# Linear attention and a top-128 expert layer on one core: the first six groups in a shorter software pipeline, the first batch's ranks from column sums, the expert's weights loaded later

## The chip, the core and the metric

The kernel runs on one core of one Trainium2 chip. The metric is the device time of one execution in microseconds; three runs of the kernel before gave 183.13, 183.86 and 184.06, the median is 183.86. The engines named below are PE (TensorE matmul; PEld is its weight load), DVE (VectorE), ACT (ScalarE), POOL (GpSimd) and SP (SyncE, which here issues most of the DMAs).

## What is computed

Four batches, eight heads, 768 rows of 64 values, all in float32. The first half is linear attention with a decay per head, in blocks of 64 rows; the second half takes its output as a row of 512 values per token, scores each token, and sends the 128 best tokens of each batch through a two-layer network whose result is added to them.

```python
# per block of 64 rows, state starts at 0
intra = einsum(q k^T) * Dmask ;  intra = einsum(intra, v)
inter = einsum(q * lam_pow, kv_state)
out   = intra + inter
kv_state = lam_block * kv_state + einsum(k * rev_pow, v)
# then, per batch, on x = out as [768, 512]
scores = x @ w_gate ;  top = the 128 highest
x[top] += sigmoid(scores[top]) * (relu(x[top] @ w1) @ w2)
```

## The kernel before, in words

The work is cut into 24 groups of 128 rows (two blocks c = 0, 1), six per batch: group g is tile t = g % 6 of batch g // 6. Each group goes through the same pieces, each a small function:

- `load(g)` issues three DMAs on SP (q, k and v, 256 KB each). A pool keeps seven groups. In the first part of the kernel `fetch_in` makes each load wait until the load three before it has landed (line 69).
- `transposes(g)` turns q and k on PE (L219, L233) into two PSUM banks, and ACT copies them to `qkT` (L224, L238, or L243 when k's half goes to the tail of the `pu` banks). `keys_decayed(g)` (L205) and `queries_decayed(g)` (L270) multiply by powers of the decay on POOL; they make `kd` and `qs`.
- `scores(g)` (L285), `from_states(g)` (L345) and `from_scores(g)` (L356) are the attention's matmuls into `po`; `masked(g)` (L292, DVE) makes `p`, which `from_scores(g)` reads. `state_products(g)` (L308) needs `kd` and fills `pu`; `next_state` adds the decayed state on DVE, either from a product that `decay_state` made on POOL (L318, then L335) or folded into four DVE instructions (L330).
- `outputs(g)` copies the result with three ACT instructions (L370, L372) and stores it (L382, on SP); batch 1 is stored later.
- `gate_scores(g)` (L395, DVE) computes the token scores from the stored row. `row(g)` turns the score column into a row (L418, PE; L421, ACT; L424, DVE), and `compare(g)` counts by DVE instructions (L434) how many tokens beat each token. `compare_older(g)` counts against the older groups of the batch.
- After a batch `plan(b)` hands out its expert work: `ranks` (L470, L475), `tokens` (L486, L492, L495), `fetch` (an indirect DMA on POOL, L509), `gate` (L519, L528), eight hidden pieces (L547), eight back pieces (L561) and `write` (L577, an indirect DMA on POOL). Each is bound by hand to a step; `counts` says how many of the 16 pieces go to each of the steps from 7 on.

The order is written out by hand, and each engine runs its own list in that order. The main loop has one step per group. In step g the kernel finishes group g (`from_scores`, `outputs`), scores group g + 1 and prepares group g + 2. There are three variants. Steps 0 to 5 begin with the transposes of group g + 2 and the score row of group g - 1, which step g then compares; step 6 does the row and comparison of group 5, then ranks, tokens and fetch of batch 0, before `masked(7)`; from step 7 on the transposes come after `state_products`, and the expert's pieces come behind them. Until step 12 a group's `kd` is made at the beginning of the step that uses it in `state_products`; from step 12 on one step earlier (line 748).

The loop that all steps share, cut:

```python
            if g + 2 < NG:
                if g <= FED:
                    keys_decayed(g + 2)
                decay_state(2 * g + 4)
            ...
            from_scores(g)
            outputs(g)
            ...
            if g % NT and lead:
                in_order(pieces)
```

The functions concerned, with their line numbers:

## Time and profile before

| what | value |
|---|---|
| median of three runs | 183.86 us |
| the profiled execution's own time | 182.03 us |
| its span in the profile | 180.2 us |
| PE, PEld, DVE, ACT, POOL busy | 149.8, 119.5, 111.5, 68.9, 96.2 us |
| mean granted TensorE clock | 0.974 |
| moved by DMA | 31.99 MB, mean 177 GB/s |

The span covers the program's instructions; the execution's time has some 1.8 us around them. "Busy" is the union of an engine's instructions. Step g below begins where `from_scores(g)` starts on PE; in this profile the steps 0 to 16 begin at 17.54, 22.05, 26.48, 30.91, 35.36, 39.06, 43.80, 51.82, 61.07, 66.91, 72.17, 77.04, 82.56, 87.75, 92.20, 99.19 and 103.67 us. The last group's step begins at 145.86, and the last expert ends at 176.

### The profile page before, as it was taken

What the parts mean: (1) busy time and instruction counts of PE and PEld (TensorE: products, weight loads), DVE (VectorE), ACT (ScalarE), POOL (GpSimd) and SP (SyncE); (2) the same over time, 40 slices, a digit from 0 to 9 for tenths busy, and PEclk for the clock granted to TensorE, in tenths of its full rate; (3) what the DMA queues carried; (4) which work ended last, traced back from release to release, by engine and by line L of the source; (5) the groups of instructions that cost most, each with busy time, mean ns of one, the idle gap of its engine ahead of it and who ended that gap; (6) DMA issues with size and microseconds to landing.
All of it is one profiled execution on the core that took longest, in us unless ns stands there. A gap on an engine that the chain in (4) does not pass through costs nothing.

```text
span 180.2 us, 8244 instructions
## 1 busy us (share of the span) xinstructions
PE 149.8 (83%) x3586; PEld 119.5 (66%) x3586; DVE 111.5 (62%) x378; ACT 68.9 (38%) x178; POOL 96.2 (53%) x100
## 2 busy tenths in 40 slices
PE   0799777776497999999977989989999997989980
PEld 0568666665386999776655668977666896459620
DVE  4814788899844445768996583589865779330010
ACT  2214555562144344644552552563343641011100
POOL 4358666945074665569786967867574600220002
PEclk9999999999859999999999999999999999999997
DMA  4999798999999998987999999989112131011001
GB/s 97 205 226 219 195 261 221 235 276 307 289 248 272 208 275 180 199 181 174 262 242 290 225 253 245 256 215 238 62 64 62 62 125 50 7 55 58 0 0 58
DMA packets 83381, 31.99 MB, mean 177 GB/s; under 512 B 75665, under 2 KB 79761, under 8 KB 83346
## 3 DMA queue, kind: packets, MB, share of 16 engines
q1 hardware_dynamic: 82560, 29.37, 67.8%
q0 software_dynamic: 640, 2.10, 3.4%
q8 instruction: 28, 0.46, 1.1%
q14 instruction: 7, 0.06, 0.1%
q10 hardware_dynamic: 146, 0.01, 0.0%
HBM read 24.12 MB, written 7.34 MB: 175 GB/s over the span
## 4 chain that ended last, share of the span: by engine, by line
PE 55%; issue 16%; DVE 14%; POOL 6%; DMA 4%; ACT 2%; POOLq 1%; ACTq 0%
PE py L561 10%; PE ph L547 9%; PE pu L308 6%; PE po L356 6%; PE po L345 5%; PE po L285 5%; DVE cmp L434 5%; PE tq L219 5%; POOL qs L270 2%; POOL decayed L318 2%; DMA qn<-in_q_dram 2%; DVE state L335 2%; DMA out_dram<-y,tok 2%; PE tqk L257 2%; DVE p L292 2%
## 5 line engine op out<-in xcount | busy, mean ns | idle before, releaser
L270 POOL TENSOR_TENSOR qs<-qkT,qpow 128x512 f32<-128x512 f32 x24 | 33.0, 1377 | 16.9 <-ACT qkT L224 9.5
L318 POOL TENSOR_TENSOR decayed<-state,decay 128x256 f32<-128x256 f32 x34 | 28.9, 849 | 23.1 <-DVE state L335 10.8
L547 PE MATMUL ph<-xsT,w_sb 128*128 128x128 f32 x256 | 31.1, 278 | 0.7 <-ACT xsT L523 0.7
L547 PEld LDWEIGHTS ph<-xsT,w_sb 128*128 128x128 f32 x256 | 29.5, 192 | 2.5 <-ACT qkT L264 1.2
L561 PE MATMUL py<-w_sb,hs 128*128 128x512 f32 x64 | 30.0, 602 | 0.1
L434 DVE TENSOR_SCALAR_CACHE_REDUCE cmp<-sc_row,sc 128x128 bf16<-128x128 f32 (+4 forms) x65 | 29.8, 503 | 0.0
L205 POOL TENSOR_TENSOR kd<-kn,kpow 128x512 f32<-128x512 f32 x24 | 25.8, 1074 | 4.9 <-DMA kn<-in_k_dram 4.9
L335 DVE TENSOR_TENSOR state<-pu,decayed 128x256 f32<-128x256 f32 x34 | 14.3, 422 | 16.3 <-ACT qkT L243 4.5
L395 DVE CUSTOM_DVE_ANT_0 xg<-x_b,wg_b 128x512 f32<-128x512 f32 x24 | 23.3, 969 | 0.0
L308 PE MATMUL pu<-vn,kd 64*64 64x64 f32 x704 | 19.3, 234 | 2.7 <-issue 1.2
L285 PE MATMUL po<-qkT 64*64 64x64 f32 x768 | 17.6, 227 | 4.1 <-issue 3.4
L292 DVE TENSOR_TENSOR p<-po,mask 128x512 f32<-128x512 f32 x24 | 16.5, 689 | 6.3 <-PE po L345 6.2
L308 PEld LDWEIGHTS pu<-vn,kd 64*64 64x64 f32 x704 | 16.4, 145 | 5.4 <-POOL kd L205 2.6
L356 PEld LDWEIGHTS po<-vn,p 64*64 64x64 f32 x768 | 14.3, 138 | 7.6 <-issue 5.7
L285 PEld LDWEIGHTS po<-qkT 64*64 64x64 f32 x768 | 15.1, 142 | 4.9 <-issue 3.8
L356 PE MATMUL po<-vn,p 64*64 64x64 f32 x768 | 17.8, 229 | 0.7 <-issue 0.7
L224 ACT COPY qkT<-tq 128x512 f32<-128x512 f32 x16 | 9.3, 584 | 23.2 <-PE tq L219 23.2
L561 PEld LDWEIGHTS py<-w_sb,hs 128*128 128x128 f32 x64 | 11.3, 191 | 10.0 <-issue 9.6
L372 ACT COPY x_b<-po 64x256 f32<-64x256 f32 x48 | 17.6, 366 | 0.6
L345 PE MATMUL po<-state,qs 64*64 64x64 f32 x704 | 17.2, 225 | 0.3 <-POOL qs L270 0.3
L219 PE MATMUL tq<-ident,qn 128*128 128x128 f32 x64 | 12.2, 322 | 5.1 <-DMA qn<-in_q_dram 5.1
L421 ACT COPY sc_row<-pb 128x128 f32<-128x128 f32 x22 | 5.9, 267 | 25.7 <-PE pb L418 25.6
(77 smaller groups left out, 182.7 us busy)
## 6 DMA issues: line engine op xcount, KB each, us to landing
qn<-in_q_dram SPq DMA_DIRECT2D x24, 256.0 KB, 4.6
kn<-in_k_dram SPq DMA_DIRECT2D x24, 256.0 KB, 4.4
vn<-in_v_dram SPq DMA_DIRECT2D x24, 256.0 KB, 4.8
out_dram<-x_b SPq DMA_DIRECT2D x18, 256.0 KB, 4.0
w_sb<-in_moe_w_dram SPq DMA_DIRECT2D x4, 512.0 KB, 5.7
w_sb<-in_moe_w_dram SPq DMA_DIRECT2D x8, 256.0 KB, 4.5
out_dram<-x_b SPq DMA_DIRECT2D x2, 768.0 KB, 6.4
xs<-out_dram,tok POOLq DMA_INDIRECT x4, 4.2
```

The costliest lines, as they stand in the source:

```text
L205: nc.gpsimd.tensor_tensor(out=kd[:], in0=loaded[g][1][:], in1=kpow[:].rearrange("p a b -> p (a b)").unsqueeze(2).broadcast_to([128, H, D]) ...
L219: nc.tensor.transpose(tq[:, hp, :], in_=loaded[g][0][:, 2 * hp : 2 * hp + 2, :], identity=ident[:])
L270: nc.gpsimd.tensor_tensor(out=qs[:].rearrange("p c a i -> p c (a i)"), in0=qkTs[g][:, :, 0].rearrange("p c a i -> p c (a i)"), in1=qpow[:] ...
L285: nc.tensor.matmul(po[half[c], hh, 1, hp, :], lhsT=qkT[half[hh], c, 1, hp, :], rhs=qkT[half[hh], c, 0, hp, :], start=True, stop=True, skip ...
L308: nc.tensor.matmul(us[g][c][half[hh], hp * D : (hp + 1) * D], lhsT=kd[half[c], h, :], rhs=vn[half[c], h, :], start=True, stop=True, skip_g ...
L318: nc.gpsimd.tensor_tensor(out=t[:], in0=states[n][:], in1=decay[:], op=ALU.mult)
L345: nc.tensor.matmul(pos[g][half[hh ^ c], hh, 0, hp, :], lhsT=qs[half[hh], c, hp, :], rhs=states[n][half[hh], hp, :], start=(hp == 0), stop= ...
L356: nc.tensor.matmul(pos[g][half[hh ^ c], hh, 0, hp, :], lhsT=p[half[c], hh, hp, :], rhs=vn[half[c], 2 * hp + hh, :], start=(hp == 0 and (2 ...
L395: nc.vector.tensor_tensor_reduce(out=xg[:], in0=x_bs[b][:, t].rearrange("p a b e -> p (a b e)"), in1=wg_b[:], scale=1.0, scalar=0.0, op0=A ...
L434: nc.vector.tensor_scalar(out=cmp[:, : cols.stop - cols.start], in0=rows_[b][:, cols], scalar1=scs[b][:, t : t + 1], scalar2=None, op0=op, ...
L547: nc.tensor.matmul(ph[:, fc % 4, :], lhsT=w1_sb[:, dc, fc * 128 : (fc + 1) * 128], rhs=keep["xsT"][:, dc, :], start=(dc == 0), stop=(dc == ...
L561: nc.tensor.matmul(py[:], lhsT=keep["hs"][:, fc, :], rhs=w2_sb[:, fc, :], start=(fc == 0), stop=(fc == NFC - 1),)
```

## The change

Steps 0 to 5 get a loop of their own. In step g group g + 1 (not g + 2) gets its transposes, decayed keys and queries, state products, scores and state matmuls; group g gets its outputs, token scores, score row and comparison, all in the same step. On PE, steps 0 to 5 now run: transposes(g + 1), from_scores(g), state_products(g + 1), scores(g + 1), from_states(g + 1), row(g). On POOL: decay_state(2g + 2), keys_decayed(g + 1), queries_decayed(g + 1). On SP each store now stands ahead of the loads of group g + 4, and the stores of groups 4 and 5 both stand ahead of the loads of group 8.

Step 6 brings the pipeline back to two groups ahead: it does all of group 7 and the preparation of group 8, with ranks and tokens of batch 0 (`slots[:2]`) and the fetch (`slots[2:]`) between them. The counts of group 5's tokens against the five older groups serve twice: instead of separate DVE counts of group 5 as an opponent, five bf16 matmuls sum the columns of the comparison table, one ACT copy takes the sums out of PSUM and one DVE instruction adds them to the ranks.

The 16 expert pieces of batch 0 move from 3, 3, 2, 2, 2, 1, 1, 1, 1 (steps 7 to 15) to 4, 4, 3, 1, 1, 1, 1, 1 (steps 7 to 14). The first 2, 2, 2 and 1 pieces of steps 7 to 10 go ahead of `state_products(g + 2)`. In step 14 the tokens and fetch of batch 1 go behind that step's piece. The first layer's weights are asked for in step 6 around group 9 (before: two in step 5, two in step 6), the second's in steps 7 and 8.

```diff
-        if 3 <= n < 3 * (NT + 3) + n_w1 or n >= 3 * (FED + 1) + n_w1 + n_w2:
+        if 3 <= n < 3 * (NT + 4) + n_w1 or n >= 3 * (FED + 1) + n_w1 + n_w2:
...
+        if b == 0 and t == NT - 1:
+            count_later(b, range(t), t - 1)
...
+    def not_beaten(cmp):
+        pw = bank([128, NT], "pw")
+        for n in range(NT - 1):
+            nc.tensor.matmul(
+                pw[:, n : n + 1], lhsT=cmp[:, n * L : (n + 1) * L], rhs=ones_b[:],
+                start=True, stop=True,
+            )
+        behind = mod.tile([128, NT], FP32, name="behind", bufs=1)
+        nc.scalar.copy(out=behind[:, : NT - 1], in_=pw[:, : NT - 1])
+        older.append(behind)
...
-                    put(s + 2, 1, tokens)
+                    put(s + 2, 15, tokens)
...
-            counts = [1, 2] if not whole else [3, 3, 2, 2, 2, 1, 1, 1, 1] if first else [3, 3, 3, 3, 4]
+            counts = [1, 2] if not whole else [4, 4, 3, 1, 1, 1, 1, 1] if first else [3, 3, 3, 3, 4]
...
+            n_mid = {at: 2, at + 1: 2, at + 2: 2, at + 3: 1} if first else {}
+                if key <= 10 * n_mid.get(step, 0):
+                    mid.setdefault(step, []).append(piece)
...
+    for g in range(NT):
+        if g < NT - 1:
+            ask(g + 4)
+        decay_state(2 * g + 2)
+        keys_decayed(g + 1)
+        transposes(g + 1)
+        queries_decayed(g + 1)
+        from_scores(g)
+        outputs(g)
+        if g == NT - 1:
+            ask(g + 4)
+        start_u(g + 1)
+        state_products(g + 1)
+        next_state(2 * g + 2)
+        scores(g + 1)
+        from_states(g + 1)
+        gate_scores(g)
...
+        if g == NT - 1:
+            table = compare_older(g)
+            masked(g + 1)
+            row(g)
+            next_state(2 * g + 3, fold=True)
+        else:
+            next_state(2 * g + 3, fold=True)
+            row(g)
+            masked(g + 1)
+        compare(g)
...
+    g = NT
+    for i in range(n_w1):
+        if i == n_w1 // 2:
+            ask(NT + 4)
+        load_weights(i)
+    ask(NT + 5)
+    decay_state(2 * g + 2)
+    keys_decayed(g + 1)
+    transposes(g + 1)
+    queries_decayed(g + 1)
+    from_scores(g)
+    outputs(g)
+    start_u(g + 1)
+    state_products(g + 1)
+    if NGR:
+        not_beaten(table)
+    next_state(2 * g + 2)
+    scores(g + 1)
+    from_states(g + 1)
+    slots = later.pop(g, [])
+    in_order(slots[:2])
+    keys_decayed(g + 2)
+    in_order(slots[2:])
+    next_state(2 * g + 3, fold=True)
+    masked(g + 1)
+    decay_state(2 * g + 4)
+    start_u(g + 2)
+    transposes(g + 2)
+    state_products(g + 2)
+    queries_decayed(g + 2)
+    next_state(2 * g + 4)
+    gate_scores(g)
+    next_state(2 * g + 5, fold=True)
...
         for piece in early.pop(g, []):
             piece()
         if g in front:
             front.pop(g)()
+        for piece in mid.pop(g, []):
+            piece()
```

## The prediction, made before the changed kernel was run

> **What bounds the kernel now.** I read the page's slices first, then the table of stretches, then the timeline of single steps.
>
> ```profile
> PE   0799777776497999999977989989999997989980
> ...
> POOL 4358666945074665569786967867574600220002
> ...
> DMA  4999798999999998987999999989112131011001
> ```
>
> Forty slices of 4.5 us. PE is the fullest engine, but slices 3 to 17 hold its gaps: the first six groups (slices 4 to 8), the stop in slice 10, and slices 17 to 22. From slice 23 (104 us) on PE is nearly full, so a delay gained or lost before step 16 (103.67) moves the end one for one. The DMA engines are full until slice 28.
>
> ```profile
> core 0: us, PE busy (x) PEld busy (x) DVE busy (x) ACT busy (x) POOL busy (x), PEclk, DMA share, GB/s
> 17.50:39.00 21.50, 16.75 (x671) 14.80 (x669) 17.93 (x57) 12.42 (x31) 14.67 (x15) 1.00 1.01 231
> 39.00:52.00 13.00, 7.85 (x258) 6.75 (x261) 9.85 (x38) 4.05 (x12) 6.14 (x7) 0.84 1.05 288
> 61.00:66.90 5.90, 5.90 (x163) 5.60 (x161) 3.18 (x9) 3.10 (x8) 3.10 (x3) 1.00 0.93 239
> 77.00:82.50 5.50, 5.08 (x127) 3.69 (x125) 3.55 (x10) 2.51 (x7) 4.08 (x5) 1.00 0.74 164
> ```
>
> Row two, steps 0 to 5: PE idle 4.75 us of 21.5, DVE the fullest. Row three, the steps around 6: PE idle 5.15 of 13. Row four, step 8: PE has no gap. Row five, step 11: nobody is full, so a loop of waits sets the pace. That loop, from the timeline:
>
> ```profile
> 75.62 1.27 POOL L270 TENSOR_TENSOR qs<-qkT,qpow 128x512 f32<-128x512 f32 x1 [2.22 <-ACT qkT L224]
> 76.85 1.18 POOL L318 TENSOR_TENSOR decayed<-state,decay 128x256 f32<-128x256 f32 x1
> 78.00 1.03 POOL L205 TENSOR_TENSOR kd<-kn,kpow 128x512 f32<-128x512 f32 x1
> 79.09 0.69 PE L308 MATMUL pu<-vn,kd 64*64 64x64 f32 x32 [0.42 <-POOL kd L205]
> 79.71 0.66 PE L219 MATMUL tq<-ident,qn 128*128 128x128 f32 x4
> 80.48 0.58 ACT L224 COPY qkT<-tq 128x512 f32<-128x512 f32 x1 [1.55 <-PE tq L219]
> 81.14 1.27 POOL L270 TENSOR_TENSOR qs<-qkT,qpow 128x512 f32<-128x512 f32 x1 [1.42 <-ACT qkT L224]
> ```
>
> From one qs to the next is 5.52 us, and PE's expert pieces stand behind the transposes, outside it. And step 6 with the step rate of steps 0 to 5:
>
> ```profile
> 29.17 1.36 DVE L395 CUSTOM_DVE_ANT_0 xg<-x_b,wg_b 128x512 f32<-128x512 f32 x1
> 30.69 0.29 PE L418 MATMUL pb<-ident,sc 128*128 128x128 f32 x1 [1.03 <-DVE sc L395]
> 37.99 0.68 DVE L395 CUSTOM_DVE_ANT_0 xg<-x_b,wg_b 128x512 f32<-128x512 f32 x1
> 48.52 0.32 PE L486 MATMUL pk<-ids,hit 128*128 128x2 bf16 x6 [1.37 <-DVE hit L475]
> 97.89 0.29 PE L486 MATMUL pk<-ids,hit 128*128 128x2 bf16 x6 [0.78 <-ACT qkT L264]
> ```
>
> PE waits 1.03 us for the token scores in each of the first steps, and 1.37 us for the hits in step 6; the last line is PE's wait in step 14 before batch 1's tokens.
>
> [...] xg takes 1.36 us beside a kd on POOL and 0.68 when POOL is idle. [...] four transposes take 0.66 us at 37.39 and 1.09 at 48.70, after two pauses of 1.48 and 1.37 us with under a microsecond of work between. [...] 75665 of 83381 packets are under 512 B, and the loads run at 231 to 239 GB/s with the engines full, the stretch with the first weights at 288.
>
> **The prologue.** Group 1's eight transposes (12.08 to 14.05) no longer stand ahead of group 0's state matmuls, nor group 1's state products and group 2's transposes (14.5 to 17.5) ahead of from_scores(0). State 1 is ready at 12.62, from_states(0) ends near 13.2, p(0) near 14.6; behind them the transposes of group 1 (2.05 at half clock) end at 15.25, and from_scores(0) starts: 15.25 instead of 17.54, 2.3 us early.
>
> **Steps 0 to 5.** The new circle, all from one step's rows at 22.05 to 23.93 and 29.17 to 33.4: from_scores and the three copies 1.88, hand-over 0.05, xg 0.61 to the next start, four folds 0.85, cmp L424 0.27, mask L292 0.69, hand-over 0.07. Sum 4.42; before, 22.05 to 26.48 is 4.43. So a step isn't shorter: the wait for the scores goes, and the copies, the fold and the mask stand in one row behind it. POOL runs decay 0.73, kd 1.04, qs 1.27 and a hand-over 0.14 behind the fold; it ends about 0.2 us after xg starts, so xg grows by 0.1 to 0.2 (full overlap would cost 0.7). I take 4.55. Group 0's step is partly at half clock, 4.85. Then 15.25 + 4.85 + 4 x 4.55 = 38.3 for step 5 (before 39.06). Step 5 puts compare_older (0.87) ahead of the mask and fold and row behind it: 4.3, so step 6 starts at 42.6; before 43.80. Gain 1.2.
>
> **Step 6.** Group 7 isn't prepared yet, and its chain hangs on the fold of step 5, now behind the mask: cmp to 42.9, folds to 43.75, POOL decay 44.6, kd(7) 45.65 (it is queued behind the decay), PE state products 46.2, L335 46.65, rank 0.22 + the subtraction 0.15 (taken from small DVE rows) + hits 0.97 = 48.0, tokens' matmuls 0.32, two small DVE rows and hand-overs to 48.75, fold 49.6, mask 50.3. Step 7 starts at 50.3, before 51.82: gain 1.5. The five bf16 matmuls are half a microsecond at most (six take 0.32) in a gap of PE, the ACT copy is beside it; their price on the path is nothing, and up to 0.8 if PE were full. The four or five 128-wide counts (0.27 each, 1.35) that they spare are real, but kd(7) comes later than the counts would have ended (45.1). PE idles 2.6 us before 46.0, so I take the half clock here as before.
>
> **Step 7.** The fetch goes out at 48.8 (before 49.51) and lands 4.2 later (median of L509), 53.0. POOL: fetch 1.14, decay 0.73, qs(8) 1.27, so from_states(8) ends at 52.7. The gate's transposes to 53.6, copy 0.58, two pieces (8 matmul records each, 24 take 2.88, so 0.96 a piece), state products and transposes 1.5, two pieces, score row: 59.9. PE stopped for 0.98 and 0.22 us in this step ("issue") with a full DMA queue; I keep 1.0: step 8 at 60.9, before 61.07, with four pieces done instead of three.
>
> **Steps 8 to 13.** Step 8 was full (5.84) and gets a piece: 6.8, to 67.7. Step 9 was full (5.26) and gets one: 6.2, to 73.9 (before 72.17). In step 10 one piece now stands ahead of the state products, so qs(12) comes 3.45 + 0.95 after its start: 78.3, before 75.62. From there the loop of 5.52 us runs twice, whatever PE is spared: 2.7 us late. The pieces taken from steps 10 and 11 lay in that loop's shade, so they give nothing back.
>
> **Steps 14 and 15.** In step 14 the piece fills PE's wait for the bank (the 0.78 above and the piece's 0.95): gain 0.95. Step 15 loses its piece (1.0), of which I count 0.75, since masks and copies remain. 2.7 - 0.95 - 0.75 = 1.0 us late at step 16.
>
> **The loads on SP.** The stores of groups 4 and 5 stand ahead of group 8's loads, which go out at 40.2 instead of 33.34. From there a store, five groups (3.93 MB) and the weights (4.19 MB) make 8.4 MB, at 239 GB/s 35 us: group 12 lands at 75, its kd is due at 73.9. Groups 9 to 11 come just in time behind pieces. I take nothing and keep +0 to +3.
>
> **Sum.** 182.03 + 1.0 = 183.0 for a profiled execution; the median stands 1.83 higher, so 183.86 + 1.0 = 184.9. About 0.5%, 0.9 us, is what a measurement of this kernel can tell from no change.
>
> **Rivals.** (1) Faster: the start's gain survives. PE stays warm through step 6 (the transposes of 2.05 take 1.04, other work 0.3: -1.3), and the early pieces fall into waits for kd (-0.95): 184.9 - 2.3 = 182.6. For it: PE's gap in step 6 is one, not two. Against: kd waits only from step 10 on. (2) Even: only one of the two, 183.9. (3) Slower by the loads: one mechanism, group 12's keys and what follows them on POOL; it decides once they land after 73.9, 1 to 3 us: 186 to 187.5. For it: DMA full until 125 us, and k landed only 1 to 4 us ahead of kd. Against: step 11's DMA share is 0.74. (4) That the order isn't as written can be set aside: it is a manual order, and the lists of each engine show it.
>
> **Chances.** Forecast 0.42 (0.32 beyond 0.5%, 0.10 within), rival 1 0.26, rival 2 0.16, rival 3 0.16. Faster 0.26, same 0.26, slower 0.48. The range takes rival 1 with 0.8 below it for xg at its short time, and rival 3: 181.8 to 187.5.
>
> **What would show it.** Step 0 near 15.3 and steps of 4.5 us; a PE gap of over 2 us in step 6 before pu, ended by kd; step 7 near 50; four ph pieces by step 8; qs(12) near 78; in step 14 no wait at pk; step 16 near 104.7. Wrong if xg stays at 1.4 in steps 0 to 5 (some 4 us more), if step 6's transposes take 0.66, or if kd waits for a DMA after step 9.

## The result, and the profile after

The changed kernel takes 192.72 us (median of four runs, 192.25 to 193.59), the kernel before, run beside it, 183.50 (182.90 to 184.06): the ratio is 1.051, 95% interval 1.045 to 1.056. The forecast was 184.9 with a range to 187.5. The side was right, the size was wrong by almost eight.

The profiled execution took 193.59 us, its span is 191.9. Its slices:

```profile
PE   0789777776667999996796777998999998989990
...
PEclk9999999999995799999999999999999999999998
DMA  4996989928899898898999999995103131021001
```

Two things are new. The DMA engines, full until slice 28 before, have a hole in slice 8 (0.2 of their time from 38 to 43 us; a slice is 4.8 us here, and the first is slice 0). And PE's gaps in the middle of the run are deeper, in slices 18 to 24 (86 to 120 us). The half clock (5 and 7 in the row of PEclk) lies in slices 12 and 13 (58 to 67 us), before in slices 10 and 11 (45 to 54).

The stretches that answer to those of before, here steps 0 to 4, 5 and 6, 7, 8, and 11:

```profile
core 0: us, PE busy (x) PEld busy (x) DVE busy (x) ACT busy (x) POOL busy (x), PEclk, DMA share, GB/s
15.74:41.33 25.59, 20.02 (x670) 16.23 (x669) 16.86 (x60) 12.70 (x30) 14.22 (x15) 1.00 0.81 190
41.33:53.80 12.47, 8.72 (x302) 7.35 (x301) 9.87 (x35) 5.29 (x13) 6.26 (x6) 1.00 0.76 187
53.80:67.31 13.51, 10.70 (x180) 9.54 (x174) 5.51 (x14) 3.11 (x10) 5.63 (x7) 0.75 1.00 256
67.31:74.39 7.08, 7.08 (x170) 6.65 (x170) 3.18 (x11) 2.99 (x9) 4.10 (x5) 1.00 0.92 249
85.37:91.22 5.85, 4.40 (x124) 3.38 (x124) 3.82 (x10) 2.65 (x8) 4.43 (x5) 1.00 0.87 192
```

A step of 0 to 4 takes 5.1 us on average (25.59 / 5), not 4.6. (Before, the same five steps are the stretch from 17.5 to 39.0 that the prediction calls steps 0 to 5.) Step 7 takes 13.51 us, at a mean clock of 0.75: half of it ran at half clock (57.57 to 64.39 us). Step 8 is full again and 1.24 longer than before; in step 11 PE idles 1.45 us.

PE's largest waits after the first load, from the table of waits (total us, times, longest):

```profile
PE pu L310 <- POOL kd L207: 4.3, 4, 1.5
PE po L287 <- issue: 3.4, 6, 1.4
PE tk L235 <- DVE cmp L426: 2.6, 6, 0.9
PE po L347 <- issue: 1.8, 2, 1.1
```

Before, the first was the score row's wait for the scores (5.7 us). It is gone as intended. In its place stand a wait of the keys' transposes for VectorE's comparison, which uses the same PSUM bank, a wait for decayed keys, and time in which PE waited for nothing that the profile shows.

Steps 5 to 7 on PE's timeline:

```profile
45.80 0.66 PE L235 MATMUL tk<-ident,kn 128*128 128x128 f32 x4 [0.95 <-DVE cmp L426]
48.44 0.79 PE L310 MATMUL pu<-vn,kd 64*64 64x64 f32 x32 [1.35 <-POOL kd L207]
51.69 0.30 PE L510 MATMUL pk<-ids,hit 128*128 128x2 bf16 x6 [1.15 <-DVE hit L499]
51.85 0.64 PE L221 MATMUL tq<-ident,qn 128*128 128x128 f32 x4
57.85 1.09 PE L543 MATMUL pt<-ident,xs 128*128 128x128 f32 x4 [1.30 <-DMA xs<-out_dram,tok]
59.62 3.78 PE L571 MATMUL ph<-xsT,w_sb 128*128 128x128 f32 x16 [0.68 <-ACT xsT L547]
63.32 1.13 PE L310 MATMUL pu<-vn,kd 64*64 64x64 f32 x32
```

The token matmuls of step 6 start at 51.69 (before 48.52), the expert's rows land at 57.85, and PE, which had paused for them, runs the first two pieces (16 matmuls) in 3.78 us; the same count takes 1.95 later in the step. Everything behind them, `pu` and the next group's transposes among it, waits.

Executions of one kernel differ by up to several us, so the ratios below leave out those more than 1.5% above the fastest of their kernel, while the medians hold all of them; where too few were left, no ratio is given.

### The profile page after: what moved, and what is told of

Read it like the earlier page. It is cut to its first block, busy times and chain, and to the rows that moved or that the text cites. A ratio compares the mean times of both kernels' runs of the same rounds, so it can differ in the third digit from the quotient of the medians.

```text
span 191.9 us, 8251 instructions
## 1 busy us (share of the span) xinstructions
PE 155.9 (81%) x3591; PEld 121.3 (63%) x3591; DVE 111.2 (58%) x379; ACT 69.4 (36%) x178; POOL 94.7 (49%) x99
## 4 chain that ended last, share of the span: by engine, by line
PE 41%; DVE 17%; issue 14%; POOL 11%; DMA 9%; ACT 4%; POOLq 1%; ACTq 0%; DVEq 0%
PE ph L571 9%; PE py L585 8%; PE pu L310 5%; POOL decayed L320 4%; DVE cmp L436 4%; PE po L347 4%; POOL qs L272 4%; DVE xg L397 3%; PE po L358 3%; POOL kd L207 3%; PE tq L221 3%; DMA xs<-out_dram,tok 3%; DMA vn<-in_v_dram 3%; PE po L287 2%; DMA qn<-in_q_dram 2%
## 5 line engine op out<-in xcount | busy, mean ns | idle before, releaser
L272 POOL TENSOR_TENSOR qs<-qkT,qpow 128x512 f32<-128x512 f32 x24 | 32.2, 1343 | 31.7 <-ACT qkT L226 19.4
L571 PE MATMUL ph<-xsT,w_sb 128*128 128x128 f32 x256 | 33.1, 288 | 1.4 <-ACT xsT L547 1.4
L571 PEld LDWEIGHTS ph<-xsT,w_sb 128*128 128x128 f32 x256 | 31.2, 201 | 2.5 <-ACT xsT L547 2.2
L436 DVE TENSOR_SCALAR_CACHE_REDUCE cmp<-sc_row,sc 128x128 bf16<-128x128 f32 (+4 forms) x63 | 28.9, 501 | 0.1
L397 DVE CUSTOM_DVE_ANT_0 xg<-x_b,wg_b 128x512 f32<-128x512 f32 x24 | 22.5, 938 | 0.7 <-ACT x_b L374 0.6
L310 PE MATMUL pu<-vn,kd 64*64 64x64 f32 x704 | 18.3, 230 | 4.7 <-POOL kd L207 4.3
L287 PE MATMUL po<-qkT 64*64 64x64 f32 x768 | 18.3, 224 | 4.1 <-issue 3.4
L310 PEld LDWEIGHTS pu<-vn,kd 64*64 64x64 f32 x704 | 15.2, 142 | 9.3 <-POOL kd L207 5.8
L347 PEld LDWEIGHTS po<-state,qs 64*64 64x64 f32 x704 | 14.8, 136 | 5.7 <-issue 3.4
L221 PE MATMUL tq<-ident,qn 128*128 128x128 f32 x64 | 11.1, 300 | 5.1 <-DMA qn<-in_q_dram 5.1
```

Of the source, the lines that this page charges most:

```text
L272: nc.gpsimd.tensor_tensor(out=qs[:].rearrange("p c a i -> p c (a i)"), in0=qkTs[g][:, :, 0].rearrange("p c a i -> p c (a i)"), in1=qpow[:] ...
L287: nc.tensor.matmul(po[half[c], hh, 1, hp, :], lhsT=qkT[half[hh], c, 1, hp, :], rhs=qkT[half[hh], c, 0, hp, :], start=True, stop=True, skip ...
L310: nc.tensor.matmul(us[g][c][half[hh], hp * D : (hp + 1) * D], lhsT=kd[half[c], h, :], rhs=vn[half[c], h, :], start=True, stop=True, skip_g ...
L347: nc.tensor.matmul(pos[g][half[hh ^ c], hh, 0, hp, :], lhsT=qs[half[hh], c, hp, :], rhs=states[n][half[hh], hp, :], start=(hp == 0), stop= ...
L397: nc.vector.tensor_tensor_reduce(out=xg[:], in0=x_bs[b][:, t].rearrange("p a b e -> p (a b e)"), in1=wg_b[:], scale=1.0, scalar=0.0, op0=A ...
L436: nc.vector.tensor_scalar(out=cmp[:, : cols.stop - cols.start], in0=rows_[b][:, cols], scalar1=scs[b][:, t : t + 1], scalar2=None, op0=op, ...
```

## First experiments: parts of the change taken out or put in alone

The change has three parts that can be separated: the order of groups 0 to 6 with the column sums (G), the expert's schedule (S: counts per step, pieces ahead of `pu`, tokens behind a piece, later write), and the loads with the weights (W). My theory was the one of the profile: the early pieces, at half clock in step 7 and ahead of `pu` in steps 8 to 10, carry most of the loss. The rival: the first groups and the late loads carry it.

**The schedule taken out** (leaves G and W):

```diff
-            counts = ... [4, 4, 3, 1, 1, 1, 1, 1] if first else ...
-            n_mid = {at: 2, at + 1: 2, at + 2: 2, at + 3: 1} if first else {}
-                    put(s + 2, 15, tokens)      # fetch: 16, write: step + 2
+            counts = ... [3, 3, 2, 2, 2, 1, 1, 1, 1] if first else ...
+            n_mid = {}
+                    put(s + 2, 1, tokens)       # fetch: 2, write: step + 1
```

> The changed kernel with the expert work scheduled as before (16 pieces spread 3,3,2,2,2,1,1,1,1, all behind the transposes; later batches' tokens and fetch ahead of the pieces; the write one step after the last piece). First six groups, column sums and weights stay changed. Theory (most of the loss from step 7 on is the pieces put ahead of pu and the transposes, at half clock in step 7): step 7 falls from 13.5 to about 10.5 us, steps 8 to 13 give back some 2.5, steps 14 to 17 some 1: about 186 us. Rival (the loss comes from the first six groups and the late loads and weights, the pieces only wait): 190 to 192 us, and step 7 stays above 12.5.

191.48 us (189.62 to 194.50), ratio 1.034 (1.025 to 1.043). Step 7 took 12.16 us without any early piece. The theory falls: taking the schedule out gives back little. It does not follow that the schedule costs little, for in this profile the decayed keys of group 12, due in step 10, wait 3.98 us for their load until 80.24 us; in the changed kernel they start at 81.14 without a wait.

**The schedule alone, in the kernel before** (the same lines the other way round):

> The kernel before with only the expert's new schedule. Theory (the pieces ahead of pu and the transposes cost by themselves): 187 to 189 us, the loss in steps 7 to 12, and step 14 gives nothing back because pb then waits for y. Rival as the prediction had it (2.7 us lost in the loop on POOL, 1.7 given back in steps 14 and 15): 184.5 us. Rival that it takes the late fetch of the changed kernel to make the pieces dear: no change, 183.5.

187.82 us (186.50 to 190.24), ratio 1.019 (1.010 to 1.028). So the schedule does cost 4.3 us when it stands alone, and yet gives back 1.2 by the medians when it is taken out. The parts hide each other.

**The pieces' place** (`n_mid = {}`; as many pieces per step, all behind the transposes):

> The changed kernel with the same number of pieces in each step (4,4,3,1,1,1,1,1), but all of them behind the transposes and the decayed queries. Theory (it is the place of the pieces that costs, not their number): step 7 falls to about 11 us, qs no longer waits for the pieces; about 188 us. Rival (too many pieces early, wherever they stand): 191 to 193 us.

190.83 us (190.55 to 191.43), ratio 1.038 (1.031 to 1.045): some 2 us of the 9 come back. Steps 8 to 14 take 41.8 us as with the pieces ahead (41.7), but here too the decayed keys of group 12 wait for their load, 3.25 us until 80.83, so the place of the pieces could not have shown more.

**Without the column sums** (`count_later(b, range(t), t)` as before; `not_beaten` and the subtraction gone):

> The changed kernel without the column sums: the first batch's groups are counted against the last one on VectorE as before (five counts of 128 columns more in step 5, some 1.35 us), and the five small matmuls, the copy and the subtraction are gone. Prediction's view (both off the path): within 0.5 us of the changed kernel, 192.7. Rival (the subtraction of 0.67 us stands on the way to the hits, the counts don't): 0.7 us faster. Rival (the counts delay the fold and with it kd of group 7): 1 to 1.4 us slower.

192.71 us (190.75 to 194.41), ratio 1.041 (1.031 to 1.051). No difference that is clear of the noise, as the prediction had it. The counts are hidden: they end at 49.07, and DVE then waits 0.82 us for group 7's state products. The subtraction took 0.67 us, not the 0.15 that I had put down, and stands on the way to the hits; without it they came 5.05 us after the step's start instead of 5.24, as they now ran beside a `kd` and took 1.54 us instead of 0.96.

## All eight combinations

The loads as before in the changed kernel (G and S are left), cut:

```diff
-            ask(g + 4)                      # steps 0 to 4
+            ask(g + 5)
+        if g == NT - 1:
+            for i in range(n_w1 // 2):
+                load_weights(i)             # the rest in step 6, ahead of group 9
...
```

> The changed kernel with SP's order of before: each group asked for five ahead in steps 0 to 4, the weights from step 5 on, no wait for the third load before on group 9. Theory (late loads are no large part: PE waited 1.3 us in step 7 for the fetched rows, kd for keys 1.2 us, after that the loads had 3 to 8 us in hand): 191 to 192.5 us. Rival (the full queue of late loads stands behind the long step 7 and the stops of PE in steps 1 to 5): 187 to 189 us, and step 7 under 11 us.

The late weights alone in the kernel before: all of w1 in step 6 with group 9 between its halves, w2 ahead of groups 11 and 12, line 69 with NT + 4.

> The kernel before with only the weights moved behind group 8 as in the change (half of w1 one step later, groups 9 to 11 between the parts). Theory (loads as such cost nothing): 183.5 to 184.5 us. Rival (the rows fetched in step 6 and groups 9 to 12 come late): 186 to 188 us, with steps 7 to 12 longer.

The first groups alone are the changed kernel with both edits above, the schedule's and the loads'; all but them is the kernel before with both:

> The changed kernel with the expert's schedule and the loads and weights both as before: what is left of the change is the new order of groups 0 to 6 and the column sums. Theory (the new order of step 6 makes the hits and so the fetch of the expert's rows come 3 us later than before, and the long step 7 with PE at half clock follows from it alone): step 7 over 11.5 us, 188.5 to 191. Rival (each part only upsets the balance a little, and the losses come from having all three at once): 184 to 186.5, with step 7 under 10.

> The kernel before with the expert's new schedule and the late weights, and its old order of groups 0 to 6. Theory (the first groups carry at least half the loss): 187 to 188.5 us, as with the new schedule alone. Rival (schedule and weights carry it all): 191 to 193.

The difference is between medians, against the kernel before, run beside each on the same chip (183.5 to 184.6). The right half comes from one profiled execution of each kernel, by the starts of `from_scores` on PE; "kd 12" is the start of the decayed keys of group 12 on POOL, with their wait for the load in brackets.

| parts in | median (extremes) | difference | ratio | profiled | step 7 starts | step 7 | steps 8-14 | 15-16 | kd 12 |
|---|---|---|---|---|---|---|---|---|---|
| none | 183.5 | 0 | 1 | 182.0 | 51.8 | 9.25 | 38.1 | 12.5 | 71.9 |
| G | 186.24 (184.65-189.09) | +1.7 | 1.012 (0.995-1.028) | 185.9 | 52.2 | 9.46 | 38.6 | 14.5 | 73.0 |
| S | 187.82 (186.50-190.24) | +4.3 | 1.019 (1.010-1.028) | 190.2 | 50.2 | 10.16 | 45.1 | 14.2 | 76.1 |
| W | 187.43 (185.04-192.55) | +2.9 | 1.019 (0.996-1.042) | 192.6 | 52.9 | 9.25 | 43.9 | 14.9 | 78.4 (3.8) |
| G, S | 191.53 (187.84-193.30) | +7.0 | - | 193.3 | 55.5 | 12.63 | 41.7 | 12.2 | 82.0 |
| G, W | 191.48 (189.62-194.50) | +7.9 | 1.034 (1.025-1.043) | 192.4 | 52.3 | 12.16 | 45.7 | 11.9 | 80.2 (4.0) |
| S, W | 193.35 (188.32-194.21) | +8.8 | - | 193.9 | 52.1 | 14.64 | 43.1 | 12.3 | 81.1 |
| all | 192.72 (192.25-193.59) | +9.2 | 1.051 (1.045-1.056) | 193.6 | 53.8 | 13.51 | 41.7 | 13.5 | 81.1 |

The right half overstates the differences: the kernel before was profiled at 182.0 us, below its median, and W at 192.6, 5 above its own. Of the four expectations above the first kept its theory; the other three went to the rival by the medians, W alone not clear of the noise.

The rows tell three things. Of the single parts only S is clear of the noise; the intervals of G and W hold 1. The three alone add up to 8.9 us, nearly the 9.2 of the whole, and each pair costs 1.0 to 3.3 more than the sum of its two, which is within the scatter. And in each of the four profiles with two or more parts step 7 takes 12 to 15 us, where one part alone leaves it at 9.3 to 10.2; whether the parts do this or the half clock is asked below.

## What the late weights do: a hole in the DMA engines

DMA share and GB/s are the last two columns. First before, then after:

```profile
38.00:42.00 4.00, 2.83 (x114) 2.37 (x114) 3.55 (x16) 2.38 (x6) 2.40 (x3) 1.00 1.12 293
42.00:44.00 2.00, 0.73 (x28) 0.48 (x23) 2.00 (x8) 0.09 (x1) 0.55 (x1) 1.00 0.98 318
```

```profile
38.00:42.00 4.00, 2.81 (x87) 2.28 (x91) 3.22 (x9) 1.43 (x3) 1.76 (x2) 1.00 0.37 102
42.00:44.00 2.00, 1.78 (x84) 1.55 (x73) 1.92 (x10) 1.11 (x4) 0.50 (x1) 1.00 0.00 0
```

In the changed kernel the loads of group 8 stand behind the store of group 5 on SP; that store waits for step 5's copies and goes out at 43.25, the first load at 43.66 (before 33.34). With w1 no longer in step 5 there is nothing else to move. From 34 to 48 us the engines move 2.32 MB where they moved 4.06. In the kernel with W alone the late keys show on POOL, as waits for DMA ahead of `kd` of groups 10 to 12:

```profile
62.76 1.04 POOL L205 TENSOR_TENSOR kd<-kn,kpow 128x512 f32<-128x512 f32 x1 [1.75 <-DMA kn<-in_k_dram]
70.13 1.04 POOL L205 TENSOR_TENSOR kd<-kn,kpow 128x512 f32<-128x512 f32 x1 [1.81 <-DMA kn<-in_k_dram]
78.37 1.04 POOL L205 TENSOR_TENSOR kd<-kn,kpow 128x512 f32<-128x512 f32 x1 [3.83 <-DMA kn<-in_k_dram]
```

If the hole is the cause and not the weights' place, it helps to ask for group 9 in step 5, ahead of the late weights:

```diff
-        ahead = 4 if g < NT - 1 else 3 if g < NT else 4 if g <= NT + 2 else 5
+        ahead = 4 if g <= NT + 2 else 5
```

> The kernel before with the late weights, but group 9 asked for in step 5, ahead of them (with the late weights alone, PE's weights move from step 5 to step 6 and the DMA engines fall to 0.12 of their time from 42 to 44 us, and kd of groups 10 to 12 waits 1.8, 1.8 and 3.8 us for keys). Theory (it is this hole that costs, not the weights' place): DMA share over 0.9 from 36 to 46 us, those waits for keys under 1 us in all, 183 to 185 us. Rival (the weights between groups 9 and 12 hold up the keys): waits as before, 187 us.

185.60 us (183.22 to 186.79), ratio 0.995 (0.987 to 1.003): no difference from the kernel before, and none of the three waits for keys is left. That the hole makes the keys late is shown by this; that it costs W its 2.9 us is not clear of the noise, as the two intervals overlap a little. From 42 to 44 us the engines are now busy, if not full:

```profile
42.00:44.00 2.00, 1.50 (x70) 1.37 (x70) 1.11 (x5) 0.06 (x1) 1.64 (x2) 1.00 0.70 161
```

The same in the changed kernel (`ask(g + 5)` in steps 0 to 5, nothing else):

> The changed kernel with the loads of groups 4 to 8 asked for one step earlier and group 9 in step 5, the weights still behind group 8 (the changed kernel's DMA engines stand at 0.37 of their time from 38 to 42 us and at nothing from 42 to 44). Theory (the hole is part of the loss, but the schedule's own steps 8 to 14 hide the late keys): DMA share over 0.9 from 36 to 46, step 7 shorter by 1 us at most, 191 to 192.5 us. Rival (the hole's 1.7 MB are what the long step 7 waits for): 188 to 190 us.

192.46 us (188.58 to 192.89), 7.9 above the kernel before beside it. The hole is gone here too (0.80 from 42 to 44 us), and nearly nothing is gained. In both kernels the decayed keys of group 12 start at about the same time without a wait, at 80.94 here and at 81.14 in the changed kernel. But the load of the next keys, which waits for those of group 12 to land, goes out at 72.51 here and only at 80.84 in the changed kernel:

```profile
80.84 0.37 SPq L67 DMA_DIRECT2D kn<-in_k_dram  x1
81.14 1.49 POOL L207 TENSOR_TENSOR kd<-kn,kpow 128x512 f32<-128x512 f32 x1
```

So in the changed kernel these keys come 0.3 us before they are used. Two limits stand there close together, the late keys and what makes step 7 long. Rival 3 of the prediction had the first of them. By the medians the loads cost 2.2 us in the whole change (7.0 without, 9.2 with them), 1.3 of it by the hole; neither is beyond the scatter.

## What the schedule does: a loop on POOL, and no relief after it

`pu` of steps 10, 11 and 12, before and after:

```profile
73.61 0.65 PE L308 MATMUL pu<-vn,kd 64*64 64x64 f32 x32
79.09 0.69 PE L308 MATMUL pu<-vn,kd 64*64 64x64 f32 x32 [0.42 <-POOL kd L205]
84.61 0.69 PE L308 MATMUL pu<-vn,kd 64*64 64x64 f32 x32 [0.41 <-POOL kd L205]
```

```profile
83.08 0.69 PE L310 MATMUL pu<-vn,kd 64*64 64x64 f32 x32
88.60 0.69 PE L310 MATMUL pu<-vn,kd 64*64 64x64 f32 x32 [1.45 <-POOL kd L207]
94.12 0.69 PE L310 MATMUL pu<-vn,kd 64*64 64x64 f32 x32 [1.28 <-POOL kd L207]
```

From the start of step 8 the first comes after 12.5 us before (73.61 - 61.07) and 15.8 after (83.08 - 67.31): two more pieces in steps 8 and 9 and one ahead of it in step 10. Then the loop runs 5.52 us twice, as predicted, and the pieces that steps 10 to 12 were spared only lengthen PE's waits from 0.4 to 1.3 or 1.45. That part of the prediction held to 0.4 us.

Step 14 did not. The token matmuls no longer wait, but the score row behind them does:

```profile
107.52 0.29 PE L510 MATMUL pk<-ids,hit 128*128 128x2 bf16 x6
108.72 0.32 PE L420 MATMUL pb<-ident,sc 128*128 128x128 f32 x1 [0.91 <-DVE y L593]
```

Batch 0's last piece now ends in step 14, and the row falls on the bank from which DVE (L593, 0.75 us) still reads that piece's result. To tell the order of tokens and piece from the place of the last piece, the order alone in the kernel before:

```diff
-                    put(s + 2, 1, tokens)       # fetch: 2
+                    put(s + 2, 15, tokens)      # fetch: 16
```

> The kernel before with one thing of the schedule: the later batches' tokens and fetch stand behind the first piece of their step, no longer ahead. The first batch's pieces are spread as before (last one in step 15). Theory (the token sums then use the other small bank, and the score row of step 14 falls on the bank that the second last piece's y is read from or waits behind it; in the changed kernel this wait took 0.91 us): step 14 stays within 0.5 us of its 6.98, 183.5 to 184.5 us. Rival as the prediction had it (the piece fills the wait for the bank): step 14 shorter by 0.9, 182.6.

185.12 us (183.71 to 186.94), ratio 0.999 (0.992 to 1.006). Step 14 takes 6.67 us, 0.3 less than before, and the row waits 0.32 us for the tokens' sum. So the order is harmless and brings a third of what I had counted; what is left as the cause is the last piece, which one step earlier than before puts its reader in the row's way. Of the eleven profiled kernels with the new schedule nine show this wait with 0.91 us and one with 0.71.

The relief of step 15 exists, and is not kept: it takes 4.33 us (before 4.48) and in the profiles of the other kernels with S 3.1 to 4.6, but steps 15 and 16 together take 12.2 to 14.2 with S and 11.9 to 14.9 without.

## Step 7: late rows, half clock

Two edits of the changed kernel aim at step 7. The first puts the column sums ahead of group 7's state products on PE, and ranks and hits ahead of its new state on DVE, where they had waited behind it until 49.33 us:

```diff
+    not_beaten(table)
+    in_order(slots[:1])
     start_u(g + 1)
     state_products(g + 1)
-    not_beaten(table)
...
-    in_order(slots[:2])
+    in_order(slots[1:2])
```

> The changed kernel with the column sums ahead of the state products of group 7 on PE, and the ranks and hits ahead of the new state of group 7 on VectorE (that state waits until 49.3 us for kd of group 7 through its products, so the hits fit before it). Nothing else moves. Theory (the hits stand behind that state; so the fetch goes out late, PE waits in step 7 and runs at half clock): hits end near 49.4 after the start of the span instead of 51.6, the fetch goes out 1.5 us earlier, PE's waits in step 7 shrink from 2.8 to about 1 us, step 7 to 10 or 11: 189.5 to 191 us. Rival (the rows' landing time is set by the full DMA queues): the fetch lands no earlier, 192.7.

192.86 us (190.67 to 194.52), ratio 1.054 (1.041 to 1.068). The hits end at 49.09 (51.63) and PE's waits in step 7 fall from 2.8 to 0.7; step 7 takes 9.44 us. But step 6 takes 8.67 (7.41), since `from_states` now waits 1.02 us for the state behind the hits and PE ran at half clock from 49 us on.

The second fills PE's two pauses of step 7 with transposes of the identity, 16 and 7 of them:

> The changed kernel with 16 transposes of the identity ahead of the gate's transposes in step 7 and 7 ahead of its first piece, whose results are overwritten: PE has work in the two pauses of step 7 (the rows' landing, the copy of their transpose). Theory (those pauses put PE at half clock: pt 1.09 us for four, two pieces 3.78 instead of 1.92, pu 1.13): pt 0.65, the two pieces 1.9 to 2.0, step 7 shorter by 2.5 us, 190 to 191 us. Rival (the pieces are slow because the weights are read beside a full load, or the throttle holds the clock): pieces stay at 3.8, no gain or up to 1 us of loss.

194.11 us (192.31 to 195.71), ratio 1.061 (1.047 to 1.074). Step 7's work runs at full pace, as the theory said:

```profile
57.82 0.60 PE L548 MATMUL pt<-ident,xs 128*128 128x128 f32 x4
58.26 0.93 PE L525 MATMUL ph<-ident 128*128 128x128 f32 x7
59.09 2.05 PE L577 MATMUL ph<-xsT,w_sb 128*128 128x128 f32 x16
61.08 0.69 PE L310 MATMUL pu<-vn,kd 64*64 64x64 f32 x32
```

The two pieces take 2.05 us instead of 3.78, step 7 takes 10.53. Yet the half clock is not gone. It now lies ahead of step 7, and step 6 took 8.33 us; the third number from the end is the mean clock:

```profile
46.00:54.50 8.50, 7.13 (x207) 6.34 (x203) 4.45 (x18) 2.80 (x7) 6.27 (x7) 0.60 0.93 228
54.50:65.00 10.50, 10.31 (x204) 9.59 (x200) 5.38 (x16) 3.31 (x9) 4.88 (x5) 1.00 0.95 238
```

The loss is the same as in the changed kernel, 3.4 us (8.5 x 0.40, there 13.51 x 0.25). The other profiles show stretches like these. From the start to 139.5 us the 20 profiles have 30 stretches at half clock, each 3.4, 6.8 or 10.2 us long at a clock of 0.50 (before and after one each, of 6.83). Half of that time is lost: per profile 0 (G alone), 1.7, 3.4 (before and after both), 5.1, 6.8 or 8.5 us (G and W). In the 3.4 us ahead of each stretch PE had been idle for some 1.4 to 2.8 us (2.30 before, 1.85 after). With the added transposes the stretch, again 6.8 us long, began at 47.17, behind 1.7 us of pauses and ahead of the added work; what sets the start and the length of a stretch is not shown.

The length of step 7 goes with where the half clock falls. In the eight profiles where a stretch begins more than 3 us after the start of step 7, over the expert's pieces, the step takes 12.1 us or more; in the other twelve it takes 10.53 or less. One of the twelve is the changed kernel with another bank for the score rows (next section), which has all three parts and no edit in step 7: its half clock lay in step 6, and its step 7 took 10.41 us.

The medians do not follow, and the record shows one reason. Where step 7 is short, the late keys take over. In the kernel with the other bank and in the one with the added transposes, step 8 starts 3.2 and 2.7 us earlier than in the changed kernel, but the decayed keys of group 12 only 0.3:

```profile
80.84 1.04 POOL L207 TENSOR_TENSOR kd<-kn,kpow 128x512 f32<-128x512 f32 x1 [2.69 <-DMA kn<-in_k_dram]
```

```profile
80.89 1.04 POOL L207 TENSOR_TENSOR kd<-kn,kpow 128x512 f32<-128x512 f32 x1 [1.62 <-DMA kn<-in_k_dram]
```

Of the gain 1.1 us is left at `pu` of step 10. With the early ranks these keys start at 77.89 us, and that execution took 190.67; why its median stands at 192.86 stays open. The times of the changed kernel's other executions agree with this reading: at a mean granted clock of 1.000, 0.999, 0.979 and 0.966 it took 192.25, 192.62, 193.59 and 192.81 us. So the half clock is not what holds the changed kernel at 192.7. No run has both edits, no hole and no half clock in step 7. Two single executions come near it: without the hole one at a clock of 0.999 took 188.58 us, and with the loads as before one at 0.998 took 187.84.

## The first groups: four waits, and one that was not seen

The next group's key transposes wait for the comparison (2.6 us in all). The score rows of groups 0 to 5 in the other bank:

```diff
-            row(g)
+            row(g, us[g + 1][0][:, NHP * D :])
```

> The changed kernel with the score rows of groups 0 to 5 written to the free part of the bank of the next group's state products, not to one of the two small banks. Theory (the transposes of the next group's keys wait 0.3 us in each of steps 0 to 4 and 0.95 in step 5 for VectorE's comparison of that row, since they share the bank): those waits go, steps 0 to 5 lose some 2.4 us in all, at most 1.5 of it kept to the end: 190.5 to 192 us. Rival (the circle through copies, fold and mask sets the step, the bank's wait hides behind it): under 0.5 us, 192.7.

192.68 us (192.17 to 193.65), ratio 1.055 (1.035 to 1.074). The rival holds: `from_scores` then waits 0.48 us a step for the mask, in the circle that the prediction had drawn, and of steps 0 to 5 mostly step 5 gets shorter (4.21 instead of 5.05).

G alone, in an execution without stops, shows what the prediction missed in steps 0 to 6. In step 4 no decay stands ahead of `kd` of group 6 (a batch begins there), so it starts beside the scores; first POOL, then DVE:

```profile
36.34 1.05 POOL L207 TENSOR_TENSOR kd<-kn,kpow 128x512 f32<-128x512 f32 x1
```

```profile
36.35 1.59 DVE L397 CUSTOM_DVE_ANT_0 xg<-x_b,wg_b 128x512 f32<-128x512 f32 x1
```

I mended this order with loads and schedule as before: a copy of one score on POOL ahead of `kd` of groups 6 and 7, that `kd` ahead of the decay in step 6, ranks before group 7's state, group 5's row in the other bank.

```diff
+        if g == NT - 1:
+            after_score(g - 1)              # gpsimd copy of the [128, 1] score
         keys_decayed(g + 1)
...
-    decay_state(2 * g + 2)
+    after_score(g - 1)
     keys_decayed(g + 1)
+    decay_state(2 * g + 2)
```

> The new order of groups 0 to 6 with schedule, loads and weights as before (the run with only the first groups), and four things mended in it: ranks and hits ahead of the new state of group 7; a copy of one score on POOL ahead of kd of groups 6 and 7, so that these wait for the score instead of running beside it; kd of group 7 ahead of the decay in step 6; group 5's score row in the other bank. Theory (what the first groups lose is these four: 0.9 us in step 4, 0.8 in step 5, 1.3 for kd in step 6, 2.5 for the fetched rows in step 7): step 4 about 4.5, step 5 about 4.3, step 6 about 6.5, step 7 starts at 49 to 50 us, fetch at 49; 182 to 183 us, below the kernel before. Rival (the fetch's landing and the loop on POOL set steps 7 to 12 whatever comes earlier): no better than the kernel before, 183.5 to 185.

186.31 us (184.77 to 189.32, six runs), ratio 1.006 (1.001 to 1.011): no version that beats the kernel before. The waits for `kd` and, in step 5, for the bank are gone, but step 7 starts at 53.65, not at 49. PE stood 6.7 us in steps 0 to 6 for nothing that the profile shows.

## The wait that the profile doesn't name

In the changed kernel's steps 1 and 2 such stops look like this:

```profile
23.94 0.50 PE L347 MATMUL po<-state,qs 64*64 64x64 f32 x17 [0.75 <-issue]
29.20 0.68 PE L347 MATMUL po<-state,qs 64*64 64x64 f32 x28 [1.06 <-issue]
```

Both lie in the middle of one run of equal matmuls that waits for nothing between them. Counting all that stands in PE's list, its weight loads and semaphore waits too, the two stops are 256 instructions apart (after 706 and 962). To tell a place in PE's list from a place in the program, 60 matmuls of one column ahead of everything, in PE's wait for the first load:

> The changed kernel with 60 matmuls of one column ahead of the first transposes, in PE's wait for the first load (120 instructions more in PE's list). Theory (the idle times that end with nothing shown lie where PE's list passes to another 256 instructions[...]): the idle times keep their distance of 256 and move to instructions that stand 120 earlier in the program (in step 1 from from_states back into the scores or the state products). The time stays within 2 us of the changed kernel. Rival (they wait for something at a fixed place, a buffer or a bank): they stay with the same instructions of each step.

213.26 us: the 60 matmuls took 25.8 us, not the few that I had meant, so the time says nothing. They added 240 instructions, with the weight loads, not 120. The stops stayed at positions 706 + 256 n of PE's list and so fell 15 or 16 instructions further on in the program: in these kernels it is the position that counts. The two profiles before and after have 15 stops of at least 0.3 us; 13 of them lie a multiple of 256 instructions from 706 (within one), and each of these ends 1.3 to 1.6 us after a packet of 16 KB has come on the DMA queue that the page lists as "q8 instruction: 28, 0.46" (packets, MB). The stops of at least 0.3 us, wherever they lie, take 6.0 us in the kernel before, 6.8 after, 10.3 in the mended one and 12.6 with W alone.

I had put this down to the full DMA queues, beside which these packets took 0.9 to 1.8 us before and after; that was an estimate. Test: the mended kernel and the kernel before, with two of the three loads of groups 4 to 8 left out (the expectations call that half).

```diff
+            if name != "kn" and 4 <= g <= 8:
+                tiles.append(third[name])   # group 3's q and v again
+                continue
```

> The mended first groups (the run before this one that copies one score on POOL), with half the loads of groups 4 to 8 left out: their q and v are those of group 3, so the computation of these five groups is another; the number of instructions on PE, POOL, DVE and ACT is the same. In the mended kernel PE stood 6.7 us in steps 0 to 6 for nothing that the profile shows, each time 256 instructions after the last, 1.3 to 1.5 us after a 16 KB packet of program had come, and these packets took 0.9 to 1.9 us beside full queues. Theory (PE's own program arrives late because the DMA queues are full): these stops shrink to under 2.5 us in steps 0 to 6, step 7 starts before 50 us. Rival (the stops are a fixed cost per 256 instructions, whatever the queues hold): they stay near 6 us, step 7 after 52.

> The kernel before with the same loads left out (q and v of groups 4 to 8 are those of group 3; the computation of these groups is another). Theory (in the kernel before PE waits for the token scores in steps 0 to 4 anyway, so its program's arrival costs less there): step 7 starts at 49.5 to 51 us, 1 to 2.5 us earlier than 51.8, less than the mended kernel gains. Rival (the queues hold up the kernel before as much): step 7 before 49.

184.99 us (181.98 to 188.16, 21 runs), ratio 0.997 (0.993 to 1.001), and 182.44 (180.63 to 184.60, 13 runs), ratio 0.989 (0.985 to 0.993). With the DMA engines at 0.45 of their time in steps 1 to 3 (0.88 with all loads), the mended kernel still stood 2.1 us in steps 1 to 4 (2.9). In step 5 the engines were nearly full again (0.89 from 40 to 44 us), so the 5.1 us of steps 0 to 6 (6.7) say less; step 7 started at 54.1. The rival fits better: full queues don't look like the main cause, by one profile of each. Both kernels gained about 1% by the lighter load (1.006 to 0.997, and 1 to 0.989); the kernel before starts step 7 at 50.6. So the mended order, whose PE has hardly another wait, has its stops where nothing hides them, while in the kernel before part of them may fall into PE's wait for the scores. That last reading is argued from the two profiles, not shown: other kernels with the old order stood up to 4.2 us in steps 0 to 4 as well.

## Why the prediction was wrong, by its own steps

The steps that failed are four: the start's gain, step 7, the gains of steps 14 and 15, and the loads, which were put at nothing. The forecast for a profiled execution was 183.0 us; it took 193.59, 10.6 more. In order of time, for this one execution:

- **Prologue and steps 0 to 6, +3.5** (step 7 at 53.80, forecast 50.3). G alone, whose profile has no such stops there, starts step 7 at 52.20: the prologue 0.45 late, step 0 0.23, steps 1 to 3 as forecast (4.42, 4.55, 4.54 for 4.55), step 4 0.89 too long (`xg` 1.59 us beside `kd`), step 5 0.76 (the bank's wait), step 6 0.3 shorter. The other 1.6 I put down to PE's stops (2.9 us in all in steps 1 to 4, part of them hidden). That POOL "ends about 0.2 us after xg starts" was right for the steps that have a decay, and I didn't look at the one that has none. The bank's wait was in no term.
- **Step 6.** Its length was right (7.41 for 7.7), and the fetch goes out 6.3 us after its start (forecast 6.2). PE kept full clock (1.00 until 57.57 us) for its transposes (0.64), as rival 1 had it and the forecast did not.
- **Step 7, +2.9.** The fetch goes out 1.1 us before step 7 starts (before 2.3), and PE has the rows 5.2 us after it, not 4.2 (that was a median; before, this very fetch took 4.9); PE waits 0.84, 1.30 and 0.68 us for `qs`, the rows and their copy. And the stretch at half clock (6.83 us) lies in step 7 whole, over the pieces, 3.4 us lost, where before half of the loss lay in step 6. The forecast had 1.0 for stops, 0.3 for the rows, the copy and no half clock.
- **Steps 8 to 13, +0.4.** The term was right: two pieces, one delayed `pu`, the loop of 5.52 twice.
- **Steps 14 and 15, +1.8.** That "the piece fills PE's wait for the bank" failed: the next instruction waits for the same pair of banks (0.91 us). Of the gains of 0.95 and 0.75 nothing was left.
- **From step 16 on, +2.0.** Mostly steps 16 and 17 (15.40 us, before 13.63), of which 1.0 is stops. The forecast had no term here.

That the side was right is in part luck: of the terms behind its 1.0 us at step 16 only the 2.7 us of steps 8 to 13 held, and most of the loss stands where the forecast had a gain or nothing.

Rival 3 had a mechanism that the forecast put at nothing, and it is there. The sum had group 8's loads "go out at 40.2" and group 12 land at 75; the loads stood behind a store that waits for step 5 and went out at 43.66, the engines had nothing to move before that, and group 12's keys landed near 80.8. In the profiled execution they were 0.3 us ahead of their use, because the half clock of step 7 had made that late too. In the five kernels with a shorter step 7, without S or with the pieces behind the transposes they are waited for, 0.2 to 4.0 us.

My reading after the profile, that the early pieces carry the loss, fell at the first run. What is shown: S costs some 4 us by itself (4.3 by the medians); the hole makes the keys late; a long step 7 goes with half clock over the pieces; and in four of the five kernels just named the keys of group 12 hold up POOL until 80.2 to 80.9 us (77.9 in the one with the early ranks), where that work starts at 71.91 in the kernel before. What stays open: how much of the 9.2 us each part carries, since G and W alone are not clear of the noise; what the whole change would take with neither hole nor half clock; and what holds the executions of which there is no profile.

## What to carry to other kernels

Before a wait is removed, ask what PE would do in that time: if it would run small matmuls, stops like those above, 256 instructions apart, may take the place of the wait (6.0 us of them before, 10.3 in the mended order; argued here, not shown). When loads are moved later, look at the queue's whole list for a stretch with nothing in it; after the hole in W alone the keys of three groups came late. And when each part of a change, taken out alone, gives nothing back, look for a second limit close behind the first: here two of them let one instruction start, at 80.8 and at 81.1 us, so that taking away either one gains little.

## What the hardware showed that I had not expected

- PE stopped 256 instructions apart in its list, for up to 2.7 us (in step 5 of the changed kernel with the loads as before); in the mended kernel with the light load it still stood 1.0 us from 31.5 us on, with the DMA engines at 0.00 of their time until 32.5.
- PE's stretches at half clock lasted 3.4, 6.8 or 10.2 us, and each began behind 3.4 us in which it had idled some 1.4 to 2.8 us (30 cases up to 139.5 us, over 20 profiles).
- A DVE instruction of 128x5 values took 0.67 us (`rank<-rank,behind`, two operations on fp32), where one of 128x1 took 0.15.
- 120 matmul records of one fp32 column at the start of the program took 25.8 us, 0.21 each; four records of 128 columns just behind them took 1.09, 0.27 each: in this run 127 columns more made 0.06 us.
